# Converting the last quarter of a weight matrix in the first layer, and its w_out tiles in single-engine steps

## The chip, the cores and the metric

One core of a Trainium2 chip. PE (TensorE) multiplies, with weight loads (PEld) beside it; DVE (VectorE) and ACT (ScalarE) work elementwise; SP (SyncE) issues nearly all DMAs, in the order in which they stand in its queue. The metric is the device time of one execution in microseconds. The four engines run their own instruction lists in order and meet at semaphores.

## The reference

Attention-like reads of `x` (4 x 8 heads x 512 x 64) against a small `state` (32 rows a head), and of the state against `x`, give 2176 rows of 512. Two layers follow, each `x @ w_in` (512 to 2048), an elementwise function, `@ w_out` (2048 to 512), all in float32:

```
x = attention(x, state)                   # 4 batches of 544 rows x 512
h = x @ w_in;   x = (h - tanh(h)) @ w_out               # layer 1
h = x @ w_in2;  x = (h * tanh(log1p(exp(h)))) @ w_out2  # layer 2 ("mish")
```

The weights reach the kernel as 64-bit words (each row is twice as long in 32-bit words): the kernel itself turns the two halves of each number into one float32.

## The kernel before

**Arithmetic.** A float32 product is made of three faster ones: each operand is split into a high part (`wh`, `gh`, `yh`: a rounding copy, ACT) and a low part (`wl`, `gl`, `yl`: a subtraction, DVE). A matmul here is 128x128 by 128x512, and work comes in sixes (two k-tiles times three products) or twelves.

**Weights.** A *conversion* (`conv_steps`, L192) takes one 128x512 tile of a weight matrix from its raw form `st`: two ACT instructions (`w` and `r`), a DVE instruction that joins them, and in layer 2, where `signed` is false, another DVE instruction for the sign. It also issues the next raw load; raw tiles have three buffers. For layer 2 the converted tiles are split and stored to DRAM, to be read back as often as needed. `w_in2` is kept in four *forms* (two tiles and two sums of their parts, for a seven-product scheme); `pieces_2i` (L264) makes them for a quarter c and one k: two conversions, one combination, four splits, seven *pieces* in all. `pieces_2o` (L291) has two pieces for each of the 16 `w_out2` tiles: the conversion, and the split with its two stores.

**Layer 1** goes through batches 0, 1, 2, the state rows and batch 3, in 68 steps (16 tiles of 128 columns a batch, 4 for the state). A step multiplies up (`up_x`, 6 matmuls), takes tanh on ACT and a subtraction on DVE, splits, and multiplies down what was made three steps before (`down_x`, 12 matmuls). Beside it `keep_pace` (L1027) runs pieces from the queue `bg` towards a goal: 45 by the step `start["s"]`, 89 by `start["2"]`, at most four a step, and only while 10 slots of SBUF are free. `bg` holds the quarters c = 0, 1, 2 (66 pieces) and, from batch 3 on, 21 pieces that prepare the operands of layer 2's first half (`pieces_y`, L705). In layer 1 the engines' lists are laid out by a scheduler, so a piece need not stand where it was called.

**Layer 2** goes through 8 groups g of 256 columns, twice (u = 0, 1), and here PE, ACT and DVE keep the order of the program. A group (L874) makes seven products m1, m6, m7, m2, m5, m3, m4 of six matmuls in three banks, and after each a *slot*: one six-matmul down product of the group before (in the first group, the three last down steps of layer 1, and nothing after them), two loads for the next group, and pieces of `bg`: two a slot in groups 0, 1 and 7, else one. Between m5 and m3 stands a DVE sum `q` of bank and m1: m3 writes into the bank that `q` reads. Each finished block goes through mish on ACT, a copy `gh` on ACT and a subtraction `gl` on DVE (`mish_lo`).

At the start of layer 2 `bg` is filled with `tail`, the 22 pieces of quarter c = 3 (14 for its forms, 8 for its four `w_out2` tiles): 14 run in group 0, 8 in group 1. What is left before group 2 is run in one go; then the raw buffers become working space.

Of the kernel before, what the change touches and what calls it, by code (L numbers as in the profile page):

```python
# [9 lines left out]
F32 = mybir.dt.float32  # L10
F32R = mybir.dt.float32r
U32 = mybir.dt.uint32
ACTF = mybir.ActivationFunctionType
ALU = mybir.AluOpType
# [58 lines left out]
def attention_moe_kernel(  # L73
# [41 lines left out]
    def get(name, dtype=F32, newest=False):  # L115
        if halves and dtype == F32:
            return halves.popleft()
        i = free.pop() if newest else free.popleft()
        return Unit(slots.tile([128, 512], dtype, tag=f"k{i}", name=name), i)
# [72 lines left out]
    def conv_steps(key):  # L192


        raw = raws.pop(key).rearrange("p (n two) -> p n two", two=2)
        lo, hi = raw[:, :, 0], raw[:, :, 1]
        w, r = get("w"), get("r")
        wu, ru = w.t.bitcast(U32), r.t.bitcast(U32)
        if signed[0]:
            AC.activation(  # L200
                out=w.t, in_=hi.bitcast(F32), func=ACTF.Prelu, scale=REBIAS, alpha=NEGATIVE
            )
        else:
            AC.activation(out=w.t, in_=hi.bitcast(F32), func=ACTF.Copy, scale=REBIAS)
        yield
        AC.activation(out=ru, in_=lo, func=ACTF.Copy, scale=7.0 * 2.0 ** -32, bias=0.49)
        load_next()
        yield
        V.scalar_tensor_tensor(
            out=wu, in0=wu, scalar=3, in1=ru, op0=ALU.logical_shift_left, op1=ALU.bitwise_or  # L210
        )
        if not signed[0]:
            V.scalar_tensor_tensor(
                out=wu, in0=hi, scalar=SIGN, in1=wu, op0=ALU.bitwise_and, op1=ALU.bitwise_or
            )
        put(r)
        yield w
# [46 lines left out]
    def pieces_2i(c, k):  # L264


        w, sums = {}, {}

        def conv(j):
            w[j] = conv32(("w2i", c, k + j * KH))  # L270

        def combine():
            a1, a2 = (w[j].t.rearrange("p (g f n) -> p g f n", g=2, f=2) for j in range(2))
            sums["s12"], sums["s34"] = get("s12"), get("s34")
            s12, s34 = (sums[x].t.rearrange("p (g f n) -> p g f n", g=2, f=2) for x in FORMS[2:])
            for o, x, y, op in (
                (s12[:, :, 0], a1[:, :, 1], a2[:, :, 1], ALU.add),
                (s12[:, :, 1], s12[:, :, 0], a1[:, :, 0], ALU.subtract),
                (s34[:, :, 0], a1[:, :, 0], a1[:, :, 1], ALU.subtract),
                (s34[:, :, 1], a2[:, :, 0], s12[:, :, 1], ALU.subtract),  # L280
            ):
                V.tensor_tensor(out=o, in0=x, in1=y, op=op)
            sums["a1"], sums["a2"] = w[0], w[1]

        def keep(x):
            d = D2I[c, x, k]
            store_split(sums[x], [d[:, :, h, :].rearrange("g p e -> p g e") for h in range(2)])

        return [lambda: conv(0), lambda: conv(1), combine] + [lambda x=x: keep(x) for x in FORMS]

    def pieces_2o(t):  # L291
        w = []
        return [
            lambda: w.append(conv32(("w2o", t))),
            lambda: store_split(w[0], [D2O[t][:, h, :] for h in range(2)]),
        ]

    def conv_w1i(c, k):
        W1I[c, k] = conv32(("w1i", c, k))
# [405 lines left out]
    def pieces_y(u):  # L705


        n0, n1 = 2 * u, 2 * u + 1
        val = {}

        def sub(name, x, y, k, into=None):
            o = val[into, k] if into else get("yt")
            V.tensor_tensor(out=o.t, in0=val[x, k].t, in1=val[y, k].t, op=ALU.subtract)
            val[name, k] = o

        def begin():
            for k in range(KH):
                for name, b, kk in (
                    ("b11", n0, k), ("b12", n1, k), ("b21", n0, k + KH), ("b22", n1, k + KH),
                ):  # L720
                    val[name, k] = Y.pop((b, kk))
                sub("t1", "b12", "b11", k)

        def keep(name, k):
            YB[u, name, k] = split(val[name, k].t, name="y")
            if name != "t2":
                put(val[name, k])

        def t3(k):
            sub("t3", "b22", "b12", k, into="b12")  # L730

        def t2(k):
            sub("t2", "b22", "t1", k)

        def t4(k):
            sub("t4", "b21", "t2", k, into="t2")

        def each(fn, *a):
            return [lambda k=k: fn(*a, k) for k in range(KH)]

        return (
            [begin] + each(keep, "b11") + each(t2) + each(keep, "t2") + each(t3)
            + each(keep, "t3") + each(t4) + each(keep, "b21") + each(keep, "t1")
            + each(keep, "b22") + each(keep, "t4")
        )
# [5 lines left out]

        return [keep]

    bg, tail = deque(), deque()

    def background(n, spare):
        while n > 0 and bg and len(free) >= spare:
# [116 lines left out]
    def group(u, g, fill, ahead, with_s, rate):  # L874


        a, b, c = (psum.tile([128, 512], F32, tag=t, name="h") for t in UB)
        fill = deque(fill)

        def slot():  # L880
            if fill:
                fill.popleft()()
            for _ in range(2):
                if ahead:
                    ahead.popleft()()
            background(rate, 0)

        def free_w(*xs):
            for x in xs:
                put(*(W2.pop((g, x, k)) for k in range(KH)))  # L890

        product(u, g, "m1", a, True)
        m1 = copy_of(a)
        slot()
        product(u, g, "m6", b, True)
        p = plus(b, m1)
        slot()
        product(u, g, "m7", c, True)
        if with_s:
            gs = s_up(g, psum.tile([128, 512], F32, tag=SB_, name="hs"))  # L900
        free_w("a1")
        slot()
        product(u, g, "m2", a, False)
        c11 = mish((0, 0), a)
        slot()
        mish_lo(*c11)
        if with_s:
            s_turn(g, gs, psum.tile([128, 512], F32, tag=TB, name="gt"))
        product(u, g, "m5", b, False)
        free_w("s12")  # L910
        q = plus(b, m1)
        h22 = plus(c, q, q)
        c22 = mish((1, 1), h22.t, h22)
        slot()
        mish_lo(*c22)
        product(u, g, "m3", b, False)
        free_w("s34")
        h12 = plus(b, m1, m1)
        c12 = mish((0, 1), h12.t, h12)
        slot()  # L920
        mish_lo(*c12)
        product(u, g, "m4", c, False)
        free_w("a2")
        h21 = plus(c, p, p)
        c21 = mish((1, 0), h21.t, h21)
        slot()
        mish_lo(*c21)
        while fill or ahead:
            slot()
# [34 lines left out]
    for c in range(4):  # L964
        for k in range(KH):
            for j in (k, k + KH):
                pending.append((("w2i", c, j), cols(w2i, c, j)))
            (bg if c < 3 else tail).extend(pieces_2i(c, k))
        for t in range(4 * c, 4 * c + 4):
            pending.append((("w2o", t), rows(w2o, t)))  # L970
            (bg if c < 3 else tail).extend(pieces_2o(t))

    side = {}

# [3 lines left out]
    def at(step, fn, back=None):  # L978

        def held():  # L980
            kept = [e.floor for e in engines]
            for e, m in zip(engines, marks[-back]):
                e.floor = m
            fn()
            for e, m in zip(engines, kept):
                e.floor = m

        side.setdefault(step, []).append(held if back else fn)
# [31 lines left out]
            at(start[b - 1] + 3 + i, f)  # L1020
    for b in (1, 2, 3):
        at(start[b] - (3 if b > 1 else 1), lambda b=b: at_a(b))
    at(start[3], lambda: bg.extend(pieces_y(0)))
    pace = [(start[1] + 8, 0), (start["s"], 45), (start["2"], 89)]
    done = [0]

    def keep_pace(i):  # L1027
# [135 lines left out]
    for j, (u, g) in enumerate(groups):  # L1163
        ahead = loads_out(g)
        if j + 1 < len(groups):
            ahead += loads_in(g + 1)
        if u and g == 0:
            background(len(bg), 0)
        if (u, g) == (0, 2):
            background(len(bg), 0)  # L1170
            send(now[0] + 1, now[0] + 1)
            widen(stage.tile([128, 1024], F32, tag="st", name="wide") for _ in range(3))
            later = pieces_y(1)
            bg.extend(pieces_ys() + later[:EARLY])
        elif (u, g) == (0, NT // 2 - 1):
            bg.extend(later[EARLY:])
        group(u, g, fill, ahead, u == 1, 2 if g in (0, 1, NT // 2 - 1) else 1)
        fill = downs(u, g, u == 1, j + 1 == len(groups))
    for f in fill:
        f()  # L1180
# [33 lines left out]
```

## Time and profile before

| | us |
|---|---|
| median of 3 runs (745.83 to 747.24) | 746.79 |
| the profiled execution | 746.52 |
| its span, first to last instruction | 744.8 |
| PE busy in it | 713.7 |
| DVE, ACT busy | 470.6, 354.6 |

The span is the time from the first to the last instruction; 1.7 us of the execution lie around it. Layer 1 ends and layer 2 begins in the slices 20 to 22 of the page's forty (18.6 us each).

### The profile page before, as it was taken

The page shows a single profiled execution, that of the slowest core. Times are in us where ns is not written, and L with a number is a line of the kernel's source. Part 1 is how long each engine was busy: PE and PEld are TensorE (multiplying, and loading weights), DVE is VectorE, ACT ScalarE, POOL GpSimd, SP SyncE. Part 2 cuts the span into 40 slices and gives each one's busy share as a digit, 9 for nine tenths or more (in the row PEclk, how much of TensorE's full clock was granted, in tenths as well). Part 3 has the DMA queues.
Part 4 walks back from the last instruction along what each step waited for, and adds up shares of the span by engine and source line. Part 5 has one row for each costly group of instructions (what it writes and reads, how often), then busy time and mean ns, then how long its engine had stood idle before and what let it go on. Part 6 is the DMA issues. An engine that isn't in the chain of part 4 may idle for free.

```text
span 744.8 us, 10543 instructions
## 1 busy us (share of the span) xinstructions
PE 713.7 (96%) x3968; PEld 570.2 (77%) x3968; DVE 470.6 (63%) x795; ACT 354.6 (48%) x631; POOL 6.6 (1%) x14
## 2 busy tenths in 40 slices
PE   8899999999999999999965999999999999999997
PEld 6467877788777898778744888888788888888886
DVE  5899654867756677793566576555753455446554
ACT  6998544566754676663544343332333332222320
POOL 0000010001000000000000000000000000000000
PEclk9999999999999999999978899999999999999999
DMA  9984110038810698616688445443776454432003
GB/s 294 315 303 147 58 56 1 1 130 263 287 59 14 213 295 265 230 53 213 200 275 267 153 142 183 152 150 98 237 254 199 141 157 126 129 112 70 1 1 128
DMA packets 66979, 118.66 MB, mean 159 GB/s; under 512 B 7280, under 2 KB 28016, under 8 KB 66928
## 3 DMA queue, kind: packets, MB, share of 16 engines
q1 hardware_dynamic: 66288, 115.89, 47.5%
q0 software_dynamic: 640, 2.10, 0.9%
q8 instruction: 31, 0.51, 0.3%
q14 instruction: 20, 0.16, 0.1%
HBM read 88.34 MB, written 29.62 MB: 158 GB/s over the span
## 4 chain that ended last, share of the span: by engine, by line
PE 85%; ACT 6%; DVE 5%; DMA 2%; issue 1%; SPq 0%; DVEq 0%; ACTq 0%
PE acc L60 46%; PE h L60 31%; PE swp L60 2%; ACT w L60 2%; PE hs L60 2%; ACT r L60 1%; PE srd L60 1%; PE xtp L60 1%; DVE wide L60 1%; DVE gl L60 1%; ACT swh L60 1%; ACT wh L60 1%; ACT wide L60 1%; DMA x<-in_x_dram 1%; DVE w L60 1%
## 5 line engine op out<-in xcount | busy, mean ns | idle before, releaser
L60 PE MATMUL h<-yh,ws 128*128 128x512 f32 x448 | 160.4, 400 | 13.7 <-DVE mt L60 8.5
L60 PE MATMUL acc<-wo,gh 128*128 128x512 f32 x544 | 169.2, 392 | 2.2 <-ACT gh L60 2.2
L60 PEld LDWEIGHTS acc<-wo,gh 128*128 128x128 f32 x544 | 102.2, 189 | 23.7 <-ACT gh L60 2.6
L60 DVE TENSOR_TENSOR wide<-acc,wide 128x512 f32<-128x512 f32 (+1 forms) x99 | 67.6, 684 | 80.4 <-PE acc L60 78.9
L60 PEld LDWEIGHTS h<-yh,ws 128*128 128x128 f32 x448 | 86.4, 193 | 33.6 <-DVE mt L60 8.9
L60 PE MATMUL acc<-wo,gl 128*128 128x512 f32 x272 | 106.8, 393 | 1.7 <-DVE gl L60 1.7
L60 PE MATMUL acc<-gh,wh 128*128 128x512 f32 x244 | 99.1, 406 | 0.0
L60 PE MATMUL acc<-gh,wl 128*128 128x512 f32 x244 | 95.4, 391 | 0.0
L60 PE MATMUL acc<-gl,wh 128*128 128x512 f32 x244 | 95.4, 391 | 0.0
L60 PE MATMUL h<-yl,ws 128*128 128x512 f32 x224 | 88.9, 397 | 0.0
L60 DVE TENSOR_TENSOR wide<-h,wide 128x512 f32<-128x512 f32 x100 | 68.8, 688 | 31.1 <-ACT wide L60 22.9
L60 DVE TENSOR_TENSOR gl<-wide,gh 128x512 fp32r<-128x512 f32 x78 | 53.8, 690 | 37.9 <-ACT gh L60 37.6
L60 ACT ACTIVATE wide<-wide 128x512 f32<-128x512 f32 x48 | 30.4, 632 | 90.1 <-DVE wide L60 90.1
L60 ACT ACTIVATE wide<-h 128x512 f32<-128x512 f32 x47 | 28.1, 597 | 91.6 <-PE h L60 87.8
L60 PEld LDWEIGHTS acc<-wo,gl 128*128 128x128 f32 x272 | 51.5, 189 | 12.9 <-DVE gl L60 2.2
L60 PEld LDWEIGHTS acc<-gh,wh 128*128 128x128 f32 x244 | 45.8, 188 | 17.2 <-issue 6.4
L60 ACT ACTIVATE gh<-wide 128x512 fp32r<-128x512 f32 x78 | 49.3, 632 | 11.5 <-DVE wide L60 9.7
L60 PE MATMUL h<-ath,swh 128*128 128x512 f32 x128 | 52.1, 407 | 1.6 <-DVE t L60 1.6
L60 PEld LDWEIGHTS acc<-gh,wl 128*128 128x128 f32 x244 | 45.8, 188 | 9.9
L60 PEld LDWEIGHTS acc<-gl,wh 128*128 128x128 f32 x244 | 45.9, 188 | 9.1 <-issue 0.8
L60 PE MATMUL h<-ath,swl 128*128 128x512 f32 x128 | 50.6, 396 | 0.1
L60 PE MATMUL h<-atl,swh 128*128 128x512 f32 x128 | 50.7, 396 | 0.0
(159 smaller groups left out, 944.0 us busy)
## 6 DMA issues: line engine op xcount, KB each, us to landing
ws<-wi SPq DMA_DIRECT2D x128, 256.0 KB, 3.4
wo<-wo SPq DMA_DIRECT2D x64, 256.0 KB, 3.7
st<-in_moe_w_in_dram SPq DMA_DIRECT2D x27, 512.0 KB, 5.6
st<-in_moe_w_out_dram SPq DMA_DIRECT2D x22, 512.0 KB, 4.6
wi<-wh SPq DMA_DIRECT2D x32, 256.0 KB, 3.6
wi<-wl SPq DMA_DIRECT2D x32, 256.0 KB, 3.8
wide<-in_moe_w_out_dram SPq DMA_DIRECT2D x10, 512.0 KB, 4.8
wo<-wh SPq DMA_DIRECT2D x16, 256.0 KB, 4.5
```

The costliest lines, as they stand in the source:

```text
L60: i = fn(*args, **kw)
```

## The change

Quarter 3's forms (14 pieces) leave `tail` and go into `bg` in layer 1, behind the `pieces_y`. The goals of `keep_pace` rise with them. Its four `w_out2` tiles stay in layer 2, each as four steps instead of two pieces: the two ACT instructions of the conversion; its two DVE instructions; the high part on ACT; the low part on DVE and the stores. Groups 0 and 1 run one step a slot.

```diff
+    def steps_2o(t):
+        v = {}
+        def first():
+            v["c"] = conv_steps(("w2o", t))
+            next(v["c"])
+            next(v["c"])
+        def large():
+            v["h"] = get("wh", F32R)
+            AC.activation(out=v["h"].t, in_=v["w"].t, func=ACTF.Copy)
+        def small():
+            l = get("wl", F32R)
+            V.tensor_tensor(
+                out=l.t, in0=v["w"].t, in1=v["h"].t.bitcast(F32), op=ALU.subtract
+            )
+            put(v["w"])
+            for h, u in enumerate((v["h"], l)):
+                stores.append((now[0], u, D2O[t][:, h, :]))
+        return [first, lambda: v.update(w=next(v["c"])), large, small]
...
-            (bg if c < 3 else tail).extend(pieces_2i(c, k))
+            (bg if c < 3 else late).extend(pieces_2i(c, k))
...
-            (bg if c < 3 else tail).extend(pieces_2o(t))
+            if c < 3:
+                bg.extend(pieces_2o(t))
+            else:
+                tail.extend(steps_2o(t))
...
-    at(start[3], lambda: bg.extend(pieces_y(0)))
-    pace = [(start[1] + 8, 0), (start["s"], 45), (start["2"], 89)]
+    at(start[3], lambda: bg.extend(pieces_y(0) + list(late)))
+    pace = [(start[1] + 8, 0), (start["s"], 52), (start["2"], 103)]
...
-        group(u, g, fill, ahead, u == 1, 2 if g in (0, 1, NT // 2 - 1) else 1)
+        group(u, g, fill, ahead, u == 1, 2 if g == NT // 2 - 1 else 1)
```

PE's list holds the same instructions in the same order as before. Three places of the other lists follow.

DVE in group 0 of layer 2, from the end of layer 1's evacuations (the copies `y`) to the sum `q` (`wide_73<-h_3770,wide_72`; `h` are the banks) and the one after it; before:

```order
L60 COPY y_3865<-acc3_3306 128x512
L60 TENSOR_TENSOR wl_3872<-wide_73,wh_3871 128x512
L60 TENSOR_TENSOR wl_3878<-wide_74,wh_3877 128x512
L60 TENSOR_TENSOR wl_3897<-wide_73,wh_3896 128x512
L60 SCALAR_TENSOR_TENSOR wide_74<-wide_74,wide_73 128x512
L60 SCALAR_TENSOR_TENSOR wide_74<-st_3221,wide_74 128x512
L60 TENSOR_TENSOR gl_3908<-wide_73,gh_3890 128x512
L60 TENSOR_TENSOR wide_73<-h_3770,wide_72 128x512
L60 TENSOR_TENSOR wide_73<-h_3771,wide_73 128x512
```

And in the changed kernel, where `q` is the first row with `h_3851`, down to the block behind m3:

```order
L60 COPY y_3931<-acc3_3353 128x512
L60 TENSOR_TENSOR wl_3953<-wide_74,wh_3937 128x512
L60 TENSOR_TENSOR gl_3955<-g_3945,gh_3947 128x512
L60 TENSOR_TENSOR wide_74<-h_3851,wide_74 128x512
L60 TENSOR_TENSOR wide_74<-h_3852,wide_74 128x512
L60 TENSOR_TENSOR gl_3978<-wide_74,gh_3966 128x512
L60 TENSOR_TENSOR wide_74<-h_3851,wide_74 128x512
L60 SCALAR_TENSOR_TENSOR w_3972<-w_3972,r_3973 128x512
L60 SCALAR_TENSOR_TENSOR w_3972<-st_3261,w_3972 128x512
L60 TENSOR_TENSOR gl_3992<-wide_74,gh_3988 128x512
```

Between the last `y` and `q` stood three splits, a conversion's two instructions and `gl`; now one split and `gl` stand there, and a conversion's two instructions follow the sum behind m3.

DVE in group 1, up to the sum `q` (`mt` from a bank and m1; `acc` are the down products); before:

```order
L60 SCALAR_TENSOR_TENSOR w_4068<-w_4068,r_4069 128x512
L60 SCALAR_TENSOR_TENSOR w_4068<-st_3801,w_4068 128x512
L60 TENSOR_TENSOR wl_4077<-w_4068,wh_4076 128x512
L60 COPY out_4097<-acc_4090 128x512
L60 SCALAR_TENSOR_TENSOR w_4103<-w_4103,r_4104 128x512
L60 SCALAR_TENSOR_TENSOR w_4103<-st_3807,w_4103 128x512
L60 TENSOR_TENSOR wl_4112<-w_4103,wh_4111 128x512
L60 TENSOR_TENSOR gl_4115<-g_4086,gh_4088 128x512
L60 TENSOR_TENSOR mt_4123<-h_3985,wide_73 128x512
```

And now:

```order
L60 TENSOR_TENSOR mt_4042<-h_4009,wide_74 128x512
L60 COPY out_4051<-acc_4044 128x512
L60 SCALAR_TENSOR_TENSOR w_4057<-w_4057,r_4058 128x512
L60 SCALAR_TENSOR_TENSOR w_4057<-st_3593,w_4057 128x512
L60 COPY out_4101<-acc_4094 128x512
L60 TENSOR_TENSOR gl_4109<-g_4090,gh_4092 128x512
L60 TENSOR_TENSOR mt_4117<-h_4009,wide_74 128x512
```

Two whole conversions with their splits stood right ahead of `q`; now one conversion's two instructions do, further up.

ACT in layer 1, where the third quarter's last `w_out2` tile is converted (the tanh of batch 3's step 3 is `t_3289<-h_3282` before, and of its step 0 `t_3173<-h_3166` now); before:

```order
L60 ACTIVATE t_3289<-h_3282 128x512
L60 ACTIVATE wide_72<-st_2966 128x512 x2
L60 ACTIVATE gh_3292<-t_3289 128x512
L60 ACTIVATE wh_3355<-wide_72 128x512
L60 ACTIVATE yh_3443<-wide_73 128x512
L60 ACTIVATE yh_3447<-wide_73 128x512
L60 ACTIVATE wide_72<-st_2974 128x512
L60 ACTIVATE wide_72<-h_3330 128x512
L60 ACTIVATE yh_3620<-wide_74 128x512
L60 ACTIVATE gh_3339<-wide_72 128x512
L60 ACTIVATE wide_72<-st_2974 128x512
```

And now (`st_2917` is that tile):

```order
L60 ACTIVATE t_3173<-h_3166 128x512
L60 ACTIVATE wh_3253<-w_3244 128x512
L60 ACTIVATE wh_3201<-w_3192 128x512
L60 ACTIVATE gh_3176<-t_3173 128x512
L60 ACTIVATE w_3257<-st_2917 128x512
L60 ACTIVATE r_3258<-st_2917 128x512
L60 ACTIVATE t_3225<-h_3218 128x512
```

The conversion stood on both sides of the tanh of batch 3's step 4 (`h_3330`); now it is done ahead of the tanh of its step 1 (`h_3218`).

## Rows read from the trace of the kernel before

**Rows 1.** The page: busy time, PE's slices, loads `ws` (us to landing)
```profile
PE 713.7 (96%) x3968; PEld 570.2 (77%) x3968; DVE 470.6 (63%) x795; ACT 354.6 (48%) x631; POOL 6.6 (1%) x14
...
PE   8899999999999999999965999999999999999997
...
ws<-wi SPq DMA_DIRECT2D x128, 256.0 KB, 3.4
```

**Rows 2.** Chain that ended last, 330 to 430: start, us, what
```profile
357.26 2.72 PE acc L60 x12
359.98 1.36 PE h L60 x6
```

**Rows 3.** PE timeline: start, us, instruction, [idle before <-releaser]
```profile
370.47 0.39 PE L60 MATMUL h<-yh,ws 128*128 128x512 f32 x1
375.47 0.79 PE L60 MATMUL h<-yh,ws 128*128 128x512 f32 x1 [4.61 <-DVE wide L60]
...
384.20 0.73 PE L60 MATMUL acc<-wo,gh 128*128 128x512 f32 x2 [2.20 <-ACT gh L60]
386.65 0.60 PE L60 MATMUL acc<-wo,gl 128*128 128x512 f32 x1 [1.72 <-DVE gl L60]
...
408.82 0.79 PE L60 MATMUL h<-yh,ws 128*128 128x512 f32 x1 [8.51 <-DVE mt L60]
...
414.10 0.45 PE L60 MATMUL h<-yh,ws 128*128 128x512 f32 x1
```

**Rows 4.** DVE timeline, groups 0 and 1 of layer 2
```profile
372.79 0.69 DVE L60 SCALAR_TENSOR_TENSOR wide<-wide 128x512 uint32<-128x512 uint32 x1 [0.73 <-ACT wide L60]
...
374.13 0.68 DVE L60 TENSOR_TENSOR gl<-wide,gh 128x512 fp32r<-128x512 f32 x1
374.73 1.41 DVE L60 TENSOR_TENSOR wide<-h,wide 128x512 f32<-128x512 f32 x2
...
408.08 0.69 DVE L60 TENSOR_TENSOR mt<-h,wide 128x512 f32<-128x512 f32 x1
```

**Rows 5.** ACT timeline, group 1 of layer 2
```profile
399.17 0.65 ACT L60 ACTIVATE w<-st 128x512 f32<-128x512 f32 x1
...
403.00 0.63 ACT L60 ACTIVATE gh<-g 128x512 fp32r<-128x512 f32 x1
403.53 0.64 ACT L60 ACTIVATE w<-st 128x512 f32<-128x512 f32 x1
```

**Rows 6.** PE's earlier waits of like length, timeline
```profile
24.91 0.60 PE L60 MATMUL h<-ath,swh 128*128 128x512 f32 x1 [1.57 <-DVE t L60]
...
69.40 1.09 PE L60 MATMUL swp<-w,sbt 64*32 64x512 f32 x16 [1.56 <-DVE w L60]
```

**Rows 7.** Busy us of each engine in stretches (PEclk: granted clock; DMA share; GB/s)
```profile
370.87:375.47 4.60, 0.00 (x1) 0.01 (x1) 3.30 (x6) 1.69 (x3) 0.00 (x0) 0.76 1.03 360
375.47:379.90 4.43, 4.43 (x11) 3.46 (x12) 1.92 (x3) 2.38 (x4) 0.00 (x0) 0.50 0.72 221
...
24.90:27.00 2.10, 2.09 (x5) 1.63 (x6) 1.60 (x4) 2.10 (x5) 0.00 (x0) 0.55 0.94 339
69.40:71.00 1.60, 1.60 (x19) 0.68 (x20) 1.60 (x4) 1.09 (x2) 0.00 (x0) 1.00 0.00 0
...
240.00:310.00 70.00, 70.00 (x506) 59.50 (x505) 49.87 (x84) 48.60 (x86) 0.00 (x0) 1.00 0.79 256
290.00:300.00 10.00, 10.00 (x56) 7.33 (x55) 8.44 (x16) 7.94 (x16) 0.00 (x0) 1.00 1.00 316
340.00:350.00 10.00, 10.00 (x46) 8.29 (x45) 2.94 (x5) 3.06 (x5) 0.00 (x0) 1.00 0.76 251
```

**Rows 8.** ACT timeline, batch 3 of layer 1
```profile
306.40 0.59 ACT L60 ACTIVATE wide<-h 128x512 f32<-128x512 f32 x1
309.29 0.63 ACT L60 ACTIVATE yh<-wide 128x512 fp32r<-128x512 f32 x1 [2.30 <-DMA wo<-wh]
...
312.83 0.60 ACT L60 ACTIVATE wide<-h 128x512 f32<-128x512 f32 x1 [0.82 <-DVE wide L60]
```

More of the change, by code (lines that the diff above doesn't have):

```diff
@@ L752, in pieces_ys @@
         return [keep]
-    bg, tail = deque(), deque()
+    bg, late, tail = deque(), deque(), deque()
     def background(n, spare):
```

## The prediction

> **What bounds the kernel now.** I began with the page. PE is busy 713.7 of 744.8 us, and nearly all it lacks lies in two of its forty slices, the ones with a 6 and a 5 where layer 1 gives way to layer 2 [rows 1]. So the question is what those two slices hold. PE's timeline there has four waits: 4.61 us ahead of m3 in group 0, 2.20 and 1.72 us ahead of the first down product of group 1, and 8.51 us ahead of m3 in group 1, together 17.04 us [rows 3]. Three of them wait for a DVE result and one for ACT.
>
> What they cost is more than their length. In the stretch after the first wait the granted clock is 0.50, the 1.2 GHz level, and matmuls come at half the pace [rows 7]. I take the whole loss from a count. A six of matmuls takes 1.36 us at full clock and a twelve 2.72, 0.2267 each [rows 2]. From the last matmul of m5 at 370.47 to the first of m4 in group 1 at 414.10 [rows 3] PE has 1 + 18 (m3, m4, m1) + 54 (nine sixes: five down products, m6, m7, m2, m5) + 12 (m3, a down product) = 85 matmuls, 19.3 us of work in 43.6. The loss is 24.4 us: 17.0 of waiting and 7.3 of low clock and run-up.
>
> Why PE waits there is seen on DVE and ACT. The first wait ends when the sum `q` is done, in the pair that begins at 374.73; ahead of it DVE had a conversion (372.79) and splits [rows 4]. The longest ends with `mt` at 408.08 [rows 4], which is again `q`, and ahead of it two whole conversions stand. ACT begins one at 399.17 and the next at 403.53 [rows 5]: a conversion made whole in a slot goes ACT, DVE, ACT, DVE and takes 4.4 us, while both engines, which here keep the program's order, hold the mish and `q` behind it. Neither engine is full; it is the order that costs.
>
> **The change, part by part.**
>
> *PE*: the same instructions in the same order. All gain or loss is in waits and clock, so I price the 24.4 us that can go and what comes in their place.
>
> *Group 0 of layer 2.* It loses 14 pieces and keeps one conversion and most of another, in single steps. I follow the new order with the old durations. m5 ends at 370.47 + 0.39 = 370.86, m2 one six earlier, at 369.5. Then come mish (0.59 for a read of a bank, [rows 8]) and `gh` (0.63, [rows 5]), to 370.8 with the hand-overs; `gl` stands ahead of `q`, so 0.69 and 0.69 [rows 4], to 372.2. m3 waits 1.3 us where it waited 4.61. The next block: the second sum to 372.9, mish and `gh` to 374.2, its `gl` to 374.9, the sum behind m3 to 375.6, mish and `gh` to 376.8. PE has done m3, m4 and the next m1 by 372.2 + 3 x 1.36 = 376.3 and waits 0.5. Its third matmul needs `gl`, which stands behind a conversion's two instructions (0.69 each) and is ready at 377.5; PE has run two matmuls from 376.8 and waits 0.2 to 0.3. In all 2.1 us of waiting instead of 8.5.
>
> *Group 1.* Sixteen steps at one a slot fill groups 0 and 1 but for the last. Each slot of group 1 also has a down product on PE, 1.36 us, so `q` has that long after m5: it needs only its own 0.69, as the `gl` ahead of it can be done earlier. I take no wait here, in place of 8.51. What hides the two conversions' work is PE's own 16 sixes, 21.8 us, against about 19 instructions of at most 0.69 us on each of DVE and ACT, 13.1. If that cover went, the price is the old wait.
>
> *The clock.* Waits of the size left occur twice elsewhere: after 1.56 us at 69.40 the granted clock stayed at 1.00, after 1.57 us at 24.91 it was 0.55 [rows 6, 7]. So a short wait costs either nothing or a stretch at 1.2 GHz: ten matmuls from 375.47 in 4.43 us instead of 2.27, 2.2 us [rows 7]. I take one half, 1.1.
>
> *The 14 pieces in layer 1.* They add 4 joins, 8 half-tile sums and 8 low parts to DVE, at most 20 x 0.69 = 13.8 us, and 16 instructions of at most 0.65 to ACT, 10.4 us; four sign instructions on DVE are gone for good. In the new lists they stand in the steps 7 to 14 of batch 3. Eight steps are 8 x 4.08 (1.36 + 2.72, [rows 2]) = 32.6 us, and the steps' own two DVE instructions 11.0, so DVE would be at 24.8 of 32.6. From 340 to 350 it was busy 2.94 of 10 [rows 7]. A down step comes three steps after its up step, 12 us, and a chain of four instructions fits in that even when some pieces are in the way. I take 0; without this cover it is 13.8.
>
> *Their DMAs.* Sixteen stores of 256 KB and the raw loads move ahead of layer 2's first loads in SP's queue, and the last stores can only go at step 14. The loads that then still have to come are those of m7 and m2; m7 starts at 359.98 + 1.36 + 2.72 = 364.1 [rows 2], and a `ws` load lands 3.4 us after its issue [rows 1]. Step 14 begins three steps before m6, at 359.98 - 3 x 4.08 = 347.7, and with 1.36 for its product and three elementwise instructions its last low part is there near 351: 10 us to spare, so 0. In turn the raw tiles that layer 2 still converts are loaded before it begins.
>
> *The pace.* The goals rise, so the earlier quarters are converted earlier too, the third quarter's last `w_out2` tile by about four steps, 16.3 us. What had to be moved from 240 to 310 is 256 GB/s x 70 us = 17.9 MB [rows 7]; now it should be done by 293.7, in 53.7 us. At 316 GB/s, what a full window (DMA share 1.00) reached [rows 7], it takes 56.6: 3 us late at the end, and ACT, which meets the raw tiles in order, late with its tanh. In the trace one tanh comes 6.43 us after the one before (306.40 to 312.83, behind a 2.30 us wait for a store, [rows 8]), 2.35 later than a step's 4.08, and PE did not wait. So the late DMA is about what the slack bears. Bounds: 0, or all of 3 plus a spell at low clock and some waits on side banks, 6; below zero nothing speaks. I take 1.5, nearer the tanh that cost nothing.
>
> The Trainium skill (DMA: Bandwidth & Descriptors, Specifications) gives about 358 GB/s as a core's limit towards HBM; by that figure the 17.9 MB are an estimated 50 us, nothing is late, and this term would be 0 and the time 1.5 us lower. The trace does not agree here: its full window reached 316.
>
> **Sum**, against the profiled execution's 746.5 (its span and 1.7 around it): 746.5 - 24.4 + 2.1 + 1.1 + 0 + 0 + 1.5 = 726.8. The median of the runs is 0.3 above the profiled one, so 727.
>
> **Rivals.**
>
> *Layer 1 gets too dense.* From the state rows into batch 3 four pieces a step run for longer than before. For it: the DMA share of 1.00 and the head-of-line position of the conversions on ACT. Against: PE never waited from 240 to 310 (70.00 of 70.00 busy, [rows 7]). If DMAs kept the average of 256 GB/s, the work would end 16.3 us late, 13 beyond what the late tanh showed to be free; half to two thirds of that on PE is 8: 735.
>
> *The long wait stays.* The tiles it stood behind are still converted in groups 0 and 1. For it: the ACT-DVE-ACT-DVE path of 4.4 us is no shorter, only spread. Against: no two parts of one stand in the same slot. If it stays, 8.5 and the low clock after it (12 matmuls from 408.82 to 414.10 in 5.3 instead of 2.7, 2.6) stay: 727 + 11 = 738.
>
> *Nothing comes of it*: the waits were for loads, and the conversions merely stood beside them. The stretch of the first wait has a DMA share of 1.03 [rows 7], which speaks for it; the releasers, all DVE and ACT, against it. 746.
>
> *Slower.* Layer 1 has two banks for up products, so a step's DVE subtraction must have read its bank before the step two later. If from the state rows on (20 steps) pieces in ACT's and DVE's lists delay each by 1.3 us beyond the slack, that is 26 us: 727 - 1.5 + 26 = 751. It decides from 1.1 us a step. For it: the lists are in order; against: eight steps leave DVE a quarter of its time.
>
> **How the numbers follow.** Forecast 0.64, 723 to 731 (no clock loss and no layer 1 term give 724.5; all three at their upper ends 731 to 732). Dense layer 1 0.20, long wait 0.07, nothing 0.05, slower 0.04. The range 723 to 737 holds the first two and part of the third. A measurement of this kernel can tell 0.2% from no change, 1.5 us: faster 0.92, same 0.04, slower 0.04.
>
> **What would show it.** Right: PE's slices at the layers' border at 9, waits there of some 2 us in all, none above 1.5, the wait for `mt` gone; granted clock 1.00 in group 1; DVE at about 8 of 10 from 322 to 350. Wrong: waits of PE between 250 and 350 for a bank that DVE or ACT has not read, ACT waiting for `st` there, or first loads of `ws` that land after 355. A wait above 4 us in group 1 would refute the step on which most of the gain rests.

## The result, and the profile after

The changed kernel takes 736.44 us (median of 4 runs, 734.83 to 738.0) against 746.47 before: a ratio of 0.9865, 95% interval 0.9837 to 0.9893. It is faster by 10 us, and half of the forecast gain didn't come. The time lies in the forecast's range only because the range was drawn to hold the rival "layer 1 gets too dense", 735; the likeliest time, 727, didn't come. The profiled run took 735.38, its span 733.6.

First the page of the changed kernel, its lines that answer to [rows 1], with the clock's slices:

```profile
PE 711.8 (97%) x3968; PEld 568.9 (78%) x3968; DVE 467.1 (64%) x791; ACT 353.7 (48%) x631; POOL 6.6 (1%) x14
...
PE   8899999999999999699999999999999999999997
...
PEclk9899999999999999899999999999999999999999
...
ws<-wi SPq DMA_DIRECT2D x128, 256.0 KB, 3.8
```

The 6 and the 5 at the layers' border are 9s now. A new 6 stands earlier, in the seventeenth slice, 293 to 312 us, and the clock has an 8 there too. The gain and the loss are thus in two places, and PE's timeline of the changed kernel has both (start, us, instruction, [idle before <-releaser]):

```profile
70.38 1.09 PE L60 MATMUL swp<-w,sbt 64*32 64x512 f32 x16 [1.56 <-DVE w L60]
...
277.79 1.16 PE L60 MATMUL swp<-w,sbt 64*32 64x128 f32 x64 [0.25 <-DVE atl L60]
286.26 0.50 PE L60 MATMUL acc<-wh,gh 128*128 128x512 f32 x1 [0.79 <-ACT wide L60]
309.97 1.09 PE L60 MATMUL ysp<-ident,ys 128*128 128x128 f32 x4 [5.83 <-DVE swl L60]
...
381.25 0.39 PE L60 MATMUL h<-yh,ws 128*128 128x512 f32 x1
382.96 0.50 PE L60 MATMUL h<-yh,ws 128*128 128x512 f32 x1 [1.32 <-DVE wide L60]
387.67 0.73 PE L60 MATMUL acc<-wo,gh 128*128 128x512 f32 x2 [0.34 <-ACT gh L60]
```

At the border, the wait ahead of m3 is 1.32 where [rows 3] had 4.61; the first down product of group 1 waits 0.34 where it waited 2.20 and 1.72; the 8.51 are gone. The cut to make is at the last matmul of m5 in group 0, which begins at 370.47 in [rows 3] and at 381.25 here. Adding its 0.39, layer 1 and the first five products end at 370.86 before and 381.64 after, 10.8 us later. From there to the end of the span it was 373.9 us and is 352.0, 21.9 less. The difference of these two is the result: 11.1 less in the span.

Of the 10.8, 1.0 is there by 70 us (70.38 against 69.40 in [rows 6]), before any instruction of the two lists differs (ACT's first differing one stands near 178 us): that is variation from run to run (the clock's other 8 stands there, in the second slice). Waits of 0.25, 0.79 and 5.83 us make 6.9. What remains is smaller waits and clock, as the windows of the changed kernel show (us, then busy us of PE, PEld, DVE, ACT, POOL; granted clock, DMA share, GB/s):

```profile
240.00:310.00 70.00, 63.13 (x472) 53.31 (x470) 49.40 (x86) 45.98 (x82) 0.00 (x0) 0.98 0.75 248
...
260.00:270.00 10.00, 10.00 (x78) 9.44 (x77) 4.75 (x7) 5.44 (x10) 0.00 (x0) 1.00 0.72 243
270.00:280.00 10.00, 9.75 (x125) 8.71 (x124) 7.34 (x14) 7.74 (x14) 0.00 (x0) 1.00 0.69 200
280.00:290.00 10.00, 9.21 (x57) 8.06 (x56) 7.70 (x15) 7.18 (x14) 0.00 (x0) 1.00 0.94 314
290.00:300.00 10.00, 10.00 (x56) 7.38 (x55) 9.95 (x18) 9.18 (x18) 0.00 (x0) 1.00 0.93 286
300.00:310.00 10.00, 4.17 (x19) 3.11 (x18) 7.36 (x13) 5.36 (x10) 0.00 (x0) 0.85 1.00 373
310.00:320.00 10.00, 10.00 (x38) 8.26 (x39) 9.07 (x16) 6.40 (x11) 0.00 (x0) 0.81 0.01 5
...
380.00:390.00 10.00, 8.34 (x35) 5.96 (x34) 6.12 (x10) 5.87 (x10) 0.00 (x0) 1.00 0.93 320
390.00:400.00 10.00, 10.00 (x46) 8.28 (x45) 5.97 (x10) 5.22 (x10) 0.00 (x0) 1.00 0.44 157
400.00:410.00 10.00, 10.00 (x46) 8.29 (x45) 7.64 (x12) 7.73 (x14) 0.00 (x0) 1.00 0.90 270
```

After the long wait the clock is at 0.81 of full speed on the mean of 10 us, 1.9 us lost. Look also at the DMA: from 240 to 310 it moved 248 GB/s x 70 us = 17.4 MB, against 17.9 in [rows 7], and then it stands still (5 GB/s). SP's timeline has the last store of the third quarter, first before, then in the changed kernel:

```profile
314.78 0.32 SPq L257 DMA_DIRECT2D wo<-wl  x1
...
306.24 0.84 SPq L257 DMA_DIRECT2D wo<-wl  x1
```

It goes out 8.5 us earlier, where the goals asked for 16.3. So the transfers ran no faster on the mean, and yet in a single window the DMA reached 373 GB/s, above the 316 that I had taken for its best. The Trainium skill (DMA: Bandwidth & Descriptors, Specifications) gives about 358 for a core; this window is above that too. Neither figure was the limit over the stretch.

What was it, then? ACT's timeline of the changed kernel, in which conversions (`w`, `r`, `wide` from `st`), tanh (`t`) and splits stand in one list:

```profile
264.14 0.66 ACT L60 ACTIVATE wide<-st 128x512 uint32<-128x512 uint32 x1 [0.19 <-DVE wl L60]
...
270.35 0.68 ACT L60 ACTIVATE r<-st 128x512 uint32<-128x512 uint32 x1 [2.16 <-DMA st<-in_moe_w_in_dram]
...
280.96 0.66 ACT L60 ACTIVATE w<-st 128x512 f32<-128x512 f32 x1 [2.11 <-DMA st<-in_moe_w_in_dram]
...
288.41 0.67 ACT L60 ACTIVATE r<-st 128x512 uint32<-128x512 uint32 x1 [0.68 <-DMA wi<-wh]
...
302.55 0.63 ACT L60 ACTIVATE yh<-wide 128x512 fp32r<-128x512 f32 x1 [1.95 <-DMA wi<-wh]
...
307.45 0.63 ACT L60 ACTIVATE gh<-t 128x512 fp32r<-128x512 f32 x1 [2.27 <-DVE t L60]
...
308.99 0.59 ACT L60 ACTIVATE ys<-acc 128x512 f32<-128x512 f32 x1
```

The chain of waits of the same kernel, over the same time (start, us, what):

```profile
264.14 0.67 ACT wide L60
264.83 5.50 DMA st<-in_moe_w_in_dram
...
274.01 0.57 ACT wide L60
274.59 6.28 DMA st<-in_moe_w_in_dram
...
295.79 6.73 DMA wi<-wh
...
306.74 0.70 DVE t L60
...
309.14 0.70 DVE swl L60
```

A raw load can be issued only when a conversion has read a raw tile: ACT ends such a read at 264.8, the load goes at 264.83, and the conversion that needs its tile runs at 270.35. In between ACT's list comes to that conversion and stands for 2.16 us, and again for 2.11. The same happens where a slot is still being stored (0.68, 1.95). All that stands behind is late, down to `ys`, the copy of the state's result at 308.99, and DVE's `swl` at 309.14; PE's transposes begin at 309.97, when both are done. These three transfers are 18.5 of the 45.8 us of this chain. The rest is mostly work of ACT and DVE: at the end ACT's `gh` waits 2.27 us for a DVE subtraction (`t`, 306.74) ahead of which DVE has five other instructions to do, and from 290 to 300 DVE is busy for 9.95 of 10 us.

### The profile page after: what moved, and what is told of

Same layout as the page of the kernel before. It is cut to its first block, busy times and chain, and to the rows that moved or that the text cites. A ratio compares the mean times of both kernels' runs of the same rounds, so it can differ in the third digit from the quotient of the medians.

```text
span 733.6 us, 10510 instructions
## 1 busy us (share of the span) xinstructions
PE 711.8 (97%) x3968; PEld 568.9 (78%) x3968; DVE 467.1 (64%) x791; ACT 353.7 (48%) x631; POOL 6.6 (1%) x14
## 4 chain that ended last, share of the span: by engine, by line
PE 79%; ACT 8%; DVE 6%; DMA 4%; issue 2%; SPq 1%; DVEq 0%; ACTq 0%
PE acc L60 43%; PE h L60 29%; DMA st<-in_moe_w_in_dram 2%; ACT r L60 2%; PE hs L60 2%; PE swp L60 1%; ACT w L60 1%; ACT gh L60 1%; DVE wide L60 1%; DVE gl L60 1%; ACT wide L60 1%; PE srd L60 1%; DVE swl L60 1%; DMA x<-in_x_dram 1%; DMA wi<-wh 1%
## 5 line engine op out<-in xcount | busy, mean ns | idle before, releaser
L60 PE MATMUL h<-yh,ws 128*128 128x512 f32 x448 | 156.9, 392 | 1.8 <-DVE wide L60 1.8
L60 PEld LDWEIGHTS h<-yh,ws 128*128 128x128 f32 x448 | 84.1, 188 | 20.6 <-DVE wide L60 3.2
L60 DVE TENSOR_TENSOR wide<-acc,wide 128x512 f32<-128x512 f32 (+1 forms) x78 | 53.2, 684 | 63.2 <-PE acc L60 62.2
L60 PE MATMUL h<-yl,ws 128*128 128x512 f32 x224 | 87.3, 390 | 0.0
L60 ACT ACTIVATE wide<-wide 128x512 f32<-128x512 f32 x45 | 28.5, 633 | 78.0 <-DVE wide L60 78.0
L60 PEld LDWEIGHTS acc<-wo,gl 128*128 128x128 f32 x272 | 51.1, 188 | 11.1 <-DVE gl L60 0.4
```

Of the source, the lines that this page charges most:

```text
L60: i = fn(*args, **kw)
```

## The experiments

Seven kernels ran. The table has for each profiled run: when m5 of group 0 ends; how long that is after the start of PE's `swp` matmuls near 70 us (69.40 in [rows 6]; 68.03 to 70.55 in these traces); what follows m5 to the end of the span (us); then the median of the runs and the ratio to the kernel before, run on the same chip, with its interval.

| kernel | m5 ends | since `swp` | from m5 on | median | ratio |
|---|---|---|---|---|---|
| before | 370.86 | 301.46 | 373.9 | 746.2 to 746.5 | |
| changed | 381.64 | 311.26 | 352.0 | 736.44 | 0.9865 [0.9837, 0.9893] |
| x1_pace | 372.83 | 304.05 | 351.9 | 726.58 | 0.9734 [0.9710, 0.9758] |
| x2_turn | 380.22 | 312.19 | 351.8 | 734.38 | 0.9845 [0.9819, 0.9870] |
| x3_steps_only | 372.01 | 301.46 | 366.9 | 739.98 | 0.9912 [0.9889, 0.9936] |
| x4_forms_only | 381.32 | 311.23 | 357.7 | 738.59 | 0.9884 [0.9852, 0.9916] |
| y2_late_only | 375.02 | 305.12 | 351.9 | 729.03 | 0.9772 [0.9758, 0.9786] |
| y5_small_stores | 375.65 | 306.64 | 351.7 | 729.25 | 0.9783 [0.9759, 0.9807] |
| y4_best | 372.45 | 302.38 | 351.3 | 724.43 | 0.9709 [0.9690, 0.9729] |

The column "since `swp`" is the one to compare layer 1 by. Two pairs have the same lists up to group 0 of layer 2, before and x3_steps_only, changed and x4_forms_only; they agree there to 0.03 us, while the column ahead of it has 1.15 and 0.32 between them. In these pairs, what varies from run to run lies ahead of the `swp`.

**x1_pace: the whole change, only the goals bent back.** 45 pieces by the state rows as before the change, 65 four steps into batch 3, and the rest late.

```diff
-    pace = [(start[1] + 8, 0), (start["s"], 52), (start["2"], 103)]
+    pace = [(start[1] + 8, 0), (start["s"], 45), (start[3] + 4, 65), (start["2"], 103)]
```

> The changed kernel with other goals for the pieces of layer 1: the first three quarters at the pace of the kernel before (45 pieces by the state rows, 65 by step 4 of batch 3), the rest spread over the last twelve steps. Theory A (the 5.8 us wait of PE for the transpose of the state rows comes from converting the third quarter four steps earlier, which lets ACT meet raw tiles and stores that have not landed): that wait goes, layer 1 ends as early as before, 726 to 729 us. Rival B (the 14 added pieces themselves are too much for ACT and DVE, wherever they stand): the time stays at 734 to 738, and the wait only moves to the last twelve steps.

726.58 us. PE's timeline of this kernel:

```profile
301.11 0.66 PE L60 MATMUL ysp<-ident,wide 128*128 128x128 f32 x4 [0.49 <-ACT wide L60]
...
358.23 0.50 PE L60 MATMUL h<-yh,ws 128*128 128x512 f32 x1 [1.54 <-DMA ws<-wi]
374.14 0.50 PE L60 MATMUL h<-yh,ws 128*128 128x512 f32 x1 [1.32 <-DVE wide L60]
378.86 0.73 PE L60 MATMUL acc<-wo,gh 128*128 128x512 f32 x2 [0.34 <-ACT gh L60]
```

The 5.83 are 0.49, and the border is the changed kernel's to a hundredth: 1.32 and 0.34. One line of numbers, with every piece still in the layer where the change put it, is worth 10 us. So most of the loss comes from when the pieces run, not from their number; layer 1 stays 2.6 longer than before (304.05 against 301.46). What it costs to run the last ones late shows too: a load of forms arrives 1.54 us late for layer 2.

**x2_turn: the state's transposes four steps later.** They are what PE waited for; if their place were the fault, moving them would free it.

```diff
-            at(len(marks), lambda: state_y(u))
+            at(len(marks) + 4, lambda: state_y(u))
```

> The changed kernel with the transpose of the state rows four steps later, all else as it was. Rival C (ACT's lag of about 6 us at that place is hurt only by this one transpose, as every other product of PE has two to three steps of slack): no wait takes its place, 727 to 729 us. Theory A (the lag is a lag of everything): PE waits 3 to 6 us for an up product's bank or a down product's operand instead, 731 to 736 us.

734.38 us. The 2 us between the medians are no gain that the runs show: the intervals overlap, and since `swp` layer 1 is no shorter (312.19 against 311.26). The wait moved, as theory A said, to the next thing that needs `ys`, a down product that wants its bank:

```profile
307.56 0.79 PE L60 MATMUL acc<-gh,wh 128*128 128x512 f32 x1 [4.96 <-ACT ys L60]
```

The place of the transposes isn't the cause; ACT as a whole is late.

**x3_steps_only: the steps for `w_out2` without the forms.** The forms' pieces stay in layer 2, two a slot in groups 0 and 1, and the goals are the old ones.

```diff
-            (bg if c < 3 else late).extend(pieces_2i(c, k))
+            (bg if c < 3 else tail).extend(pieces_2i(c, k))
-    pace = [(start[1] + 8, 0), (start["s"], 52), (start["2"], 103)]
+    pace = [(start[1] + 8, 0), (start["s"], 45), (start["2"], 89)]
-        group(u, g, fill, ahead, u == 1, 2 if g == NT // 2 - 1 else 1)
+        group(u, g, fill, ahead, u == 1, 2 if g in (0, 1, NT // 2 - 1) else 1)
```

> One half of the change alone: the forms of the fourth quarter stay in layer 2 at two pieces a slot, only the four w_out tiles are made in single steps (two a slot). Layer 1 is as before, without the transpose's wait. If the forms in group 0 make the first three waits and the w_out tiles the 8.5 us one, the first three (8.5 us and some 4 of low clock) stay, and of the long one a part: 737 to 743 us.

739.98 us. PE's timeline:

```profile
376.62 0.79 PE L60 MATMUL h<-yh,ws 128*128 128x512 f32 x1 [4.61 <-DVE wide L60]
385.36 0.73 PE L60 MATMUL acc<-wo,gh 128*128 128x512 f32 x2 [2.36 <-ACT gh L60]
387.81 0.80 PE L60 MATMUL acc<-wo,gl 128*128 128x512 f32 x1 [1.72 <-DVE gl L60]
401.92 0.50 PE L60 MATMUL h<-yh,ws 128*128 128x512 f32 x1 [0.49 <-DVE mt L60]
```

The waits of group 0 in [rows 3] are back, but the 8.51 of group 1 are 0.49: those belong to the whole conversions of `w_out2`. Waits of 0.56, 0.96 and 0.69 us follow, from 411 to 426. Layer 1 stays short. This half of the change gives 373.9 - 366.9 = 7.0 us behind the cut.

**x4_forms_only: the forms in layer 1 with the changed goals, the `w_out2` tiles whole.**

```diff
-            if c < 3:
-                bg.extend(pieces_2o(t))
-            else:
-                tail.extend(steps_2o(t))
+            (bg if c < 3 else tail).extend(pieces_2o(t))
```

> The other half alone: the forms go to layer 1 with the new goals, the w_out tiles are converted whole, one piece (half a tile) a slot. If spreading alone is enough, it equals the changed kernel, 734 to 738 us; if the path ACT, DVE, ACT, DVE inside a slot costs, waits of 1 to 3 us stand before m3 in groups 0 and 1, 738 to 743 us. The transpose's wait in layer 1 stays.

738.59 us. PE's timeline:

```profile
309.56 1.09 PE L60 MATMUL ysp<-ident,ys 128*128 128x128 f32 x4 [5.42 <-DVE swl L60]
...
383.76 0.50 PE L60 MATMUL h<-yh,ws 128*128 128x512 f32 x1 [2.44 <-DVE mt L60]
390.88 0.73 PE L60 MATMUL acc<-wo,gh 128*128 128x512 f32 x2 [2.75 <-ACT gh L60]
392.73 0.80 PE L60 MATMUL acc<-wo,gl 128*128 128x512 f32 x1 [1.11 <-DVE gl L60]
```

A wait of 2.44 us stands ahead of m3 in group 0, as the second reading said. In group 1 there is none ahead of m3, and the 8.51 are gone here too: at one piece a slot, seven of the eight pieces of the tiles stand in group 0, and the price is paid there and at the first down product. This half gives 373.9 - 357.7 = 16.2 behind the cut, and carries the whole loss ahead of it (311.23 since `swp`). The halves' gains, 16.2 + 7.0 = 23.2, come to 1.3 more than the 21.9 of both together; each is from one trace, and x4's has a stretch of low clock (0.83 from 390 to 400, 1.7 us), so how much they overlap is not settled.

**y2_late_only: of x1's two bends only the first.**

```diff
-    pace = [(start[1] + 8, 0), (start["s"], 52), (start["2"], 103)]
+    pace = [(start[1] + 8, 0), (start["s"], 45), (start["2"], 103)]
```

> Of the two changes to the pace in the run at 726.6 us, only one: 45 pieces by the state rows as before the change, then one even rate up to 103 at the second layer's start, so that the rows of batch 3 get more pieces per slot than in the changed kernel (58 in place of 51). Theory P (what costs is the earlier goal, seven pieces more ahead of the state rows, which leaves ScalarE behind when batch 3 begins): 726 to 729 us, the wait ahead of the state's transposes (5.83 in the changed kernel) under 1.5. Theory D (what costs is the rate in batch 3's own rows): 735 to 739 us, a wait of 5 us or more among batch 3's rows.

729.03 us, just at theory P's upper end, though its rows of batch 3 are denser than the changed kernel's. The wait ahead of the transposes is 0.20, as P said, but one of 2.19 stands ahead of it. And the 0.20 is not quite the same place: the scheduler put the transposes 26 matmuls further back in PE's list than in x1 and in the changed kernel. Its timeline:

```profile
307.35 0.50 PE L60 MATMUL h<-ath,swh 128*128 128x512 f32 x1 [2.19 <-DVE wide L60]
310.67 0.66 PE L60 MATMUL ysp<-ident,wide 128*128 128x128 f32 x4 [0.20 <-ACT wide L60]
```

So seven pieces too early ahead of the state rows are worth 7.4 of the 9.9 us by the medians (736.4 to 729.0), and 6.1 of 7.2 by the column since `swp`. The rest, 2.4 or 1.1, would be the rate at batch 3's start; y2's interval and x1's meet at 0.9758, so its size isn't settled.

**y5_small_stores: the changed kernel with its stores cut to an eighth.** Every instruction on PE, DVE and ACT stays where it is.

```diff
...
-                out=d, in_=v if len(d.shape) == 2 else v.rearrange("p (g e) -> p g e", g=2)
-            )
+                out=d, in_=v if len(d.shape) == 2 else v.rearrange("p (g e) -> p g e", g=2)
+            ) if d is not None else nc.sync.dma_start(out=junk.popleft()[:, :], in_=v[0:16])
...
```

> The changed kernel with most of its stores cut to an eighth: the forms of w_in for quarters 2 to 4 and of w_out for tiles 4 to 15 store 16 of their 128 partitions into scratch, and the second layer loads the first quarter's forms in their place (so its output is not the reference's). Every conversion, every instruction on the three compute engines and the slots' order stay. Theory M (ScalarE falls behind because raw loads and slots that are still being stored arrive late on a full DMA): the wait ahead of the state's transposes (5.83) under 1.5, group 0's last product at 371 to 374 us on the trace (381.6 in the changed kernel), 724 to 728 us. Theory E (the engines' own work per slot is too much): the wait stays at 4 to 6, group 0's last product at 379 to 382, 734 to 737 us.

729.25 us. Neither theory comes out whole: the cut at m5 is 375.65, between the two bands, and a wait of 2.20 is left. Its timeline:

```profile
304.24 1.02 PE L60 MATMUL ysp<-ident,ys 128*128 128x128 f32 x4 [2.20 <-DVE swl L60]
```

And its windows:

```profile
300.00:310.00 10.00, 7.80 (x30) 6.16 (x30) 10.00 (x17) 6.66 (x12) 0.00 (x0) 0.83 0.05 11
304.00:306.00 2.00, 1.76 (x7) 1.60 (x8) 2.00 (x5) 1.22 (x3) 0.00 (x0) 0.58 0.00 0
```

Since `swp`, the changed kernel's layer 1 is 7.2 us longer than x1's (311.26 - 304.05). With the three engines' lists as they were, the lighter transfers take back 4.6 of them (to 306.64). Raw loads of `w_in2` landed in 4.4 us (median from 255 to 300 us) in place of 5.6, and ACT's waits for them shrank from 2.16 and 2.11 to 1.2 and 0.2. In the kernel before the same median is 5.8: its loads were no quicker, they were wanted later. The other 2.6 speak for theory E: with next to no DMA to wait for, DVE is busy for all of 300 to 310. How much of the 4.6 is late raw loads and how much slots still being stored stays open: a kernel with light loads and whole stores wasn't tried.

**y4_best: x1 with two small moves.** The goal of 103 is reached a slot earlier, for the late load; and a mish's low part goes behind `q`.

```diff
-        mish_lo(*c11)
...
         h22 = plus(c, q, q)
+        mish_lo(*c11)
-    pace = [(start[1] + 8, 0), (start["s"], 52), (start["2"], 103)]
+    pace = [(start[1] + 8, 0), (start["s"], 45), (start[3] + 4, 65), (start["2"] - 1, 103)]
+    pace.append((start["2"], 103))
```

> The run at 726.6 us with two small moves: the pace reaches 103 pieces one slot earlier, and batch c11's low product pair in a group stands behind q and h22, for more distance from the VectorE result that the first rows wait for. If the waits left at the border (1.54 for a load of forms, 1.32 for VectorE) are time on the path and nothing takes their place: 724 to 726 us. If they only pass to the next row: 726 to 728 us. If reaching the goal a slot earlier crowds batch 3 again: 729 to 733 us.

724.43 us (723.09 to 725.7), the fastest of all. The 1.54 are gone and the 1.32 are 0.78, which its timeline shows beside what is left:

```profile
302.61 0.66 PE L60 MATMUL ysp<-ident,wide 128*128 128x128 f32 x4 [0.66 <-ACT wide L60]
373.23 0.50 PE L60 MATMUL h<-yh,ws 128*128 128x512 f32 x1 [0.78 <-DVE wide L60]
377.94 0.73 PE L60 MATMUL acc<-wo,gh 128*128 128x512 f32 x2 [0.32 <-ACT gh L60]
```

It is clear of the changed kernel. All its runs lie below 726, where the second reading began. Against x1 the medians differ by 2.1 us, and the traces from `swp` to the end by 2.3, near the 1.54 and 0.54 that went; but the two intervals overlap (0.9729 and 0.9710), so how much the two moves bring is not settled.

## Why the prediction was right and wrong

*The loss at the border, 24.4 us: right.* The forecast put 2.1 of waiting and 1.1 of clock in its place, a gain of 21.2; behind the cut it is 21.9. Every kernel with both halves of the change has 351 to 352 us there, whatever layer 1 did.

*Group 0: right, nearly to the number.* 1.32 ahead of m3 for a forecast of 1.3; 0.34 at the first down product for 0.5 and 0.2 to 0.3. Following the new order with the old durations was enough.

*Group 1, no wait: right.* PE is busy for all of 390 to 410. x3 shows that the steps alone take the 8.51 away; x4, that whole conversions spread out do too, at the price of waits in group 0.

*The clock, 1.1: nothing came.* It stayed at 1.00 behind the 1.32, one of the two outcomes that the term averaged.

*The 14 pieces in layer 1, 0: right as far as x1 tells.* With all of them in layer 1, its PE waits nowhere for DVE or ACT between the 0.49 at 301 and the 1.32 ahead of m3.

*Their DMAs, 0: right in the changed kernel, which was late anyway.* With layer 1 at its old length, in x1, it is 1.54: the 10 us to spare weren't there.

*The pace, 1.5 with bounds 0 and 6: this is the step that failed.* It is the term that was mis-sized: 10.8, less the 1.0 that was there by 70 us, is 9.8, above the upper bound. Three readings in it were wrong.

First, 316 GB/s was not what a full window reaches: the first row of [rows 7] has 360 at a share of 1.03. So my sentence that the trace does not agree with the Trainium skill's figure of about 358 (DMA: Bandwidth & Descriptors, Specifications) was wrong. By that figure the term is 0, which is further off.

Second, I let the DMA catch up at that rate, "3 us late at the end". It kept its old average, 248, and the last store of the third quarter went out 8.5 us earlier instead of 16.3, some 8 late. What held the transfers up changes on the way. From 260 to 280 the DMA share is 0.72 and 0.69, so there was bandwidth; there the chain goes from a load to the conversion that waits for it and on to the next load, 5.50 and 6.28 us each. From 280 to 310 the share is 0.93 to 1.00, and one store takes 6.73. By y5_small_stores the transfers together are worth 4.6 of the 7.2 us that the goals cost; that the other 2.6 are the engines' own work is argued from a busy DVE, not shown.

Third, I took one late tanh that PE had borne [rows 8] as the measure of the slack. Here four waits of ACT for DMA, one behind the other, make 6.9 us, and PE's waits made 6.9. In y5_small_stores ACT's waits for DMA are 1.18, 0.22 and 0.30, and PE's is 2.20. That fits waits that add up before they reach PE.

*The rival "layer 1 gets too dense"* had the time, 735, from half to two thirds of 13; 9.8 came. That it came so near is in part luck: its lateness, 16.3, was about twice what came, more of it reached PE than it said, 16.3 less the 2.35 of the late tanh is 14 and not 13, and its 735 counts the 1.5 of the pace as well as the 8. Its doubt, PE never waiting in [rows 7], told little: with no wait to be seen, ACT's slack may have been large or nearly gone, and by y2_late_only seven pieces more were enough to use it up. So the chance of 0.20 for it was too small for a case whose premise was only that the average rate stays as it is.

*The signs.* Those of being right at the border came; DVE, forecast at about 8 of 10 from 322 to 350, was at 7.55, 4.51 and 7.97 in the three windows from 320 on. The signs of being wrong in layer 1 came too: PE's 5.83 us ended with a DVE instruction that reads a bank (`swl<-swp`), ACT waited 2.16 and 2.11 us for `st`, and the first `ws` load, issued at 354.3 (3.8 us to landing is the page's median), landed after 355.

## What to carry to other kernels

Work that is moved into a "free" stretch has to be fed there: before raising its rate, follow one buffer around its ring (issue, landing, use, release) and compare the time per turn with the new rate. Here the mean bandwidth and the best window told little about it. And when a change shows a gain in one place and a loss in another, cut the two traces at a common instruction between them, and count from one behind the stretch that varies from run to run: the gain was here as forecast, and one line of goals brought back most of the loss.

## What the runs showed of the hardware

One core's DMA moved 373 GB/s over 10 us, well above the 316 of [rows 7] at the same DMA share of 1.00. So the share alone doesn't tell what is moved.

Two waits of like length again differed in what the clock did after them, as in [rows 6]: behind 2.20 us in y5_small_stores it was 0.58 in the next 2 us (the window of 304 to 306 above), behind 2.19 us in y2_late_only it stayed at 1.00, as that kernel's window shows:

```profile
307.00:309.00 2.00, 1.65 (x7) 1.39 (x8) 1.26 (x3) 1.13 (x3) 0.00 (x0) 1.00 0.95 263
```

Which of the two comes, the length of the wait alone doesn't tell.
